# A chunked scan feeding two MLPs on one core: the second half of a piece's scan ahead of the next piece's first half

## The chip, the cores and the metric

The kernel runs on one core of a Trainium2 chip. The metric is device time of one execution in microseconds (us). Before the change three executions gave 623.71, 623.90 and 626.47 us, median 623.9.

## What is computed

The reference has three layers. The first is a decaying linear-attention scan over 768 steps for 4 batches and 8 heads, with state 16 x 32, in chunks of 32 steps:

```python
L = np.exp(cum[:, :, :, None] - cum[:, :, None, :]) * causal
M = np.einsum('bhin,bhjn->bhij', Cc, Bc) * L
y_intra = np.einsum('bhij,bhjd->bhid', M, xc)
y_inter = np.einsum('bhin,bhnd->bhid', Cc, state) * np.exp(cum)[:, :, :, None]
y[:, :, sl] = y_intra + y_inter
state = decay_full[:, :, None, None] * state + np.sum(Bx, axis=2)
```

Its output, as 3072 tokens of 256 features, goes through two MLPs of width 2048, `leaky_relu(x @ w_in) @ w_out` with slope 0.01 and `relu(x @ w_in)**2 @ w_out`. The weights come in as 64-bit floats.

## The kernel before, in words

**Pieces, blocks and weights.** The scan is cut into 12 pieces of 256 steps, three per batch (NPC, NP). Products run on split operands (a high and a low part, three products for one). The first MLP takes its tokens in blocks (BLOCKS, line 36): six blocks of one piece, then three of two. Block b needs yh and yl of its piece, written by the last step of that piece's scan (lines 422 and 423). A block of one piece runs in eight chunks of two rows of w1i: `hmm` issues 12 matmuls (lines 443 to 445), `act` has ScalarE write g and t (466, 467) and VectorE the low part of g (468), and `omm` issues 12 more (485, 486, 491), two chunks later (LAG). There are three g buffers and three PSUM tiles for hmm.

A weight tile goes through five steps: a load on SP's queue (117, into the pool "st" of seven buffers), two ScalarE passes (126, 129), two on VectorE (137, 139), one on ScalarE (161) and one on VectorE (162). `w_step` issues one step for each of four tiles in flight; the two tensors of the first MLP, w1i and w1o, are eight tiles each and come first, then w2i and w2o.

**The scan of a piece has two halves,** written as generators that yield after each small step.
- `scan_a(p)` (336): for the first batch scales from sums of squares (253, 308, 316 to 321, 264 to 283); him and ch on ScalarE (344, 345); `decays`, clips and a scan on VectorE (204 to 209); kmx and its diagonal copy kbd, xh (351, 354); cl (356); `from_start`, a second scan (214) and dec on ScalarE (215); xl and the copy of xh (361); the products S (368, 369), lines 370 and 373, the copy of xl; then mk (378).
- `scan_b(p)` (381): mkh and the carried state (384, 225), mkl and qh (389, 390), ql (392), the products Y (397 to 399), the states (401, 231), their parts and a transpose (406 to 410), the copy sbd, the last products (418, 419), yh and yl (422, 423).

A diagonal copy (`diag`, 328) of every piece but the first is four DMAs on SP's queue.

**What sets the order.** `stage(k)` (593) runs scan_a of piece k, scan_b of piece k-1 and, in stages 2, 5 and 8, `sequence_scales` of the next batch (287), which loads five tiles "all" into the pool "st" and has ScalarE square them. The three take turns step by step (601, 602), except in stage 1, where scan_b(0) comes whole first (597). The fourth round also emits the loads of the next piece (605), two DMAs on SP. `stages_to(x)` (612) draws steps until stage and step count, a stage being counted as 15 steps, reach x. Ahead of the blocks the kernel draws to 1 + 13.5/15 and issues eight weight steps (618 to 620); within them each chunk draws to `due(pos + 2)` (651), which makes stage p0 + n + 1 due four chunk halves ahead of a block (623) and spreads the steps at RATE. Stage k holds the last step of piece k-1.

The order of the text is not the order on an engine: a list scheduler puts instructions on each engine's queue, the earlier in the text first among those it takes to be ready. On the chip each queue then runs in that order.

Of the kernel before, what the change touches and what calls it, by code (L numbers as in the profile page):

```python
# [24 lines left out]
NP = BATCH * NPC  # L25
# [5 lines left out]
KI, KO = DM // P, FF // P  # L31
# [9 lines left out]
RATE = 1.4 / KO  # L41
LEAD = 4
NSTEP = 15
NHEAP = 24


# [5 lines left out]
def ssd_moe_kernel(ctx: ExitStack, tc: tile.TileContext, in1, in2, w1i, w1o, w2i, w2o, out):  # L52
# [10 lines left out]
    sm = ctx.enter_context(tc.tile_pool(name="sm", bufs=2))  # L63
    heap = ctx.enter_context(tc.tile_pool(name="heap", bufs=NHEAP))
    ap_ = ctx.enter_context(tc.tile_pool(name="ap", bufs=2))
# [126 lines left out]
    def load_piece(p):  # L192
        v = sp.tile([P, U * (N + T + D)], F32, tag="in1", name="in1", bufs=2)
        w = sp.tile([P, U * 2 * T], F32, tag="in2", name="in2", bufs=2)
        nc.sync.dma_start(v, in1[p])
        nc.sync.dma_start(w, in2[p])
        return part(v, N + T, D), part(v, 0, N), part(w, T, T), part(v, N, T), part(w, 0, T), part(w, 0, T + N)
# [89 lines left out]
    def sequence_scales(s):  # L287

        mx = sm.tile([P, 5], F32, tag="mx", name="mx")
        all_ = in1[NPC * s : NPC * s + NPC].rearrange("a p f -> p a f")  # L290

        for to, at in ((0, N + T), (3, N + T + 16), (1, N), (4, N + 16), (2, 0)):
            t = big([P, NPC, U * 16], F32, "all", "st", 7)
            nc.sync.dma_start(t, all_[:, :, U * at : U * (at + 16)])
            yield
            squares(mx[:, to : to + 1], t)
            yield
        sc, isc, sbp = yield from powers(mx, 5)

        fac = sm.tile([P, 1], F32, tag="fac", name="fac")  # L300
        nc.vector.tensor_tensor(fac, isc[:, 0:1], isc[:, 2:3], ALU.mult)
        nc.vector.scalar_tensor_tensor(fac, fac, 1.0 / KK, isc[:, 1:2], ALU.mult, ALU.mult)
        for p in range(NPC * s, NPC * s + NPC):
            scales[p] = sc[:, 0:1], sc[:, 2:3], sc[:, 1:2], sbp, fac, KK, 1.0
# [121 lines left out]
    blocks, q0 = [], 0  # L426
# [158 lines left out]
    def piece_y(p):  # L585
        return lambda: tuple(t[:, p % 2] for t in y_of(p))
# [6 lines left out]
    def stage(k):  # L593
        a = scan_a(k, loaded.pop(k)) if k < NP else iter(())
        b = scan_b(k - 1, piece_y(k - 1)) if k > 0 else iter(())
        bd = sequence_scales(k // NPC + 1) if k % NPC == NPC - 1 and k + 1 < NP else iter(())
        if k == 1:
            yield from b
        n = 0
        live = [b, a, bd]  # L600
        while live:
            live = [g for g in live if next(g, g) is not g]
            n += 1
            if n == 4 and k + 1 < NP:
                loaded[k + 1] = load_piece(k + 1)
            yield

    sc_it = (k for k in range(NP + 1) for _ in stage(k))
    now = [0, 0]
    cum = []  # L610

    def stages_to(x):
        while now[0] < NP + 1 and now[0] + min(now[1] / NSTEP, 0.99) < x:
            k = next(sc_it, NP + 1)
            now[:] = (k, now[1] + 1) if k == now[0] else (k, 0)

    stages_to(1)
    stages_to(1 + 13.5 / NSTEP)
    for _ in range(8):
        w_step()  # L620


    starts = [(KO * p0 - LEAD, p0 + n + 1) for p0, n in blocks[1:]]

    def due(at):
        return max(nb - max(RATE * (b - at), 0) for b, nb in starts)
# [16 lines left out]
    for i, (p0, n) in enumerate(blocks):  # L643
        ph_ = One(p0, n)
        for m in range(0, KO, 2 // n):
            ms = list(range(m, m + 2 // n))
            need("1i", m // 2)
            ph_.hmm(ms)
            pos += 2
            ph_.act(ms)  # L650
            stages_to(due(pos + 2))
            pend.append((ph_, ms, ms[-1] == KO - 1))
            if len(pend) > LAG[n]:
                need("1o", pend[0][1][-1] // 2)
            second(LAG[n])
            first_w = wq[:1] and wq[0][0][0] == "1" or any(v[0][0] == "1" for v in w_loaded + w_half + w_full)
            acc += 1.0 if first_w else (0.3 if i < len(blocks) - 1 else 1.5)
            while acc >= 1:
                acc -= 1
                (w_step if first_w else w_one)()  # L660
            if i == len(blocks) - 1 and m == KO - 4:
                split_y(0)
        if p0 % 2 + n == 2:
            ys.pop(p0 // 2)
# [68 lines left out]
```

## Time and profile before

| | us |
|---|---|
| three executions | 623.71, 623.90, 626.47 |
| profiled execution | 623.66 |
| its span, first to last instruction | 621.9 |
| TensorE busy | 574.2 |
| VectorE busy | 462.8 |
| ScalarE busy | 450.8 |
| mean granted clock of TensorE | 0.979 |

PE is TensorE, PEld its weight loads, DVE VectorE, ACT ScalarE, POOL GpSimd, SP the queue that issues the DMAs. Lines like L162 are lines of the kernel. A wait is idle time of an engine, put down to the operand that came last. The granted clock is a share of full speed.

### The profile page before, as it was taken

To read this page: it belongs to the slowest core of one execution; us is meant where nothing else is said; L and a number is where in the kernel's file an instruction comes from. 1 tells how busy PE (TensorE), PEld (TensorE's weight loads), DVE (VectorE), ACT (ScalarE), POOL (GpSimd) and SP (SyncE) were. 2 spreads that over 40 slices of the span, in tenths; PEclk is the share of its full clock that TensorE was granted. 3 is DMA by queue.
4 is the path that set the end of the run, shared out by engine and by line. 5 is a ranking of instruction groups with operands and counts; after the bars stand their busy time and mean duration, and the time that the engine had idled before them with its cause. 6 is when DMAs were issued, how large, how long until landed. Compare 5 with 4: busy or idle time off the path is not lost.

```text
span 621.9 us, 11809 instructions
## 1 busy us (share of the span) xinstructions
PE 574.2 (92%) x4674; PEld 521.6 (84%) x4674; DVE 462.8 (74%) x782; ACT 450.8 (72%) x723; POOL 5.2 (1%) x15
## 2 busy tenths in 40 slices
PE   0284889999999999999999999999999999999996
PEld 0274889899999978888888889989999999999996
DVE  6999799876688867645847457786787777777765
ACT  6996798766867765545666578877877878777773
POOL 3000000000000000000000000000000000000000
PEclk9985889999999999999999999999999999999999
DMA  8657766267357633202301000010010000100101
GB/s 322 211 130 225 231 184 156 28 155 236 47 110 199 185 65 53 28 10 52 87 24 35 0 2 2 0 35 1 1 34 1 9 27 1 35 1 1 35 1 35
DMA packets 113575, 46.52 MB, mean 75 GB/s; under 512 B 94448, under 2 KB 103280, under 8 KB 113520
## 3 DMA queue, kind: packets, MB, share of 16 engines
q1 hardware_dynamic: 113520, 45.76, 27.8%
q8 instruction: 37, 0.61, 0.4%
q14 instruction: 18, 0.15, 0.1%
HBM read 36.83 MB, written 3.15 MB: 64 GB/s over the span
## 4 chain that ended last, share of the span: by engine, by line
PE 83%; DVE 10%; ACT 3%; DMA 1%; issue 1%; DVEq 0%; ACTq 0%
PE hp L443 13%; PE hp L444 13%; PE hp L445 13%; PE o L485 4%; PE oo L485 4%; PE o L564 4%; PE o L491 4%; PE o L486 3%; PE o L562 3%; PE o L563 3%; PE oo L486 3%; PE oo L491 3%; PE Ym L564 3%; PE Ym L563 3%; PE Ym L562 3%
## 5 line engine op out<-in xcount | busy, mean ns | idle before, releaser
L443 PE MATMUL hp<-yl,w1i 128*128 128x256 f32 (+1 forms) x288 | 94.8, 329 | 9.1 <-DVE yl L423 6.4
L468 DVE TENSOR_TENSOR g<-t,g 128x512 fp32r<-128x512 f32 x96 | 65.7, 685 | 42.2 <-ACT t L467 39.7
L540 DVE TENSOR_TENSOR tl<-ts,th 128x1024 fp32r<-128x1024 f32 x48 | 58.8, 1225 | 49.2 <-ACT th L538 49.2
L445 PE MATMUL hp<-yh,w1i 128*128 128x256 f32 (+1 forms) x288 | 94.0, 326 | 0.0
L444 PE MATMUL hp<-yh,w1i 128*128 128x256 f32 (+1 forms) x288 | 93.8, 326 | 0.0
L466 ACT ACTIVATE g<-hp 128x512 fp32r<-128x512 f32 x96 | 57.2, 596 | 38.8 <-PE o L491 25.8
L528 ACT ACTIVATE b<-hp 128x512 f32<-128x512 f32 x96 | 57.2, 596 | 35.4 <-PE hp L445 35.4
L443 PE MATMUL hp<-xl,w2i 128*128 128x512 f32 x192 | 75.3, 392 | 0.0
L444 PE MATMUL hp<-xh,w2i 128*128 128x512 f32 x192 | 75.2, 392 | 0.0
L445 PE MATMUL hp<-xh,w2i 128*128 128x512 f32 x192 | 74.7, 389 | 0.0
L443 PEld LDWEIGHTS hp<-yl,w1i 128*128 128x128 f32 x288 | 56.8, 197 | 13.5 <-issue 4.0
L538 ACT CAST th<-ts 128x1024 fp32r<-128x1024 f32 x48 | 50.2, 1047 | 15.8 <-DVE ts L537 15.6
L445 PEld LDWEIGHTS hp<-yh,w1i 128*128 128x128 f32 x288 | 56.8, 197 | 3.7
L444 PEld LDWEIGHTS hp<-yh,w1i 128*128 128x128 f32 x288 | 56.8, 197 | 3.6
L485 PE MATMUL oo<-g,w1o 128*128 128x256 f32 x192 | 51.9, 300 | 8.3 <-DVE w1o L162 8.3
L467 ACT ACTIVATE t<-hp 128x512 f32<-128x512 f32 x96 | 57.3, 597 | 0.0
L529 ACT ACTIVATE b<-b 128x1024 f32<-128x1024 f32 x48 | 50.9, 1061 | 1.1
L486 PE MATMUL oo<-g,w1o 128*128 128x256 f32 x192 | 50.6, 293 | 0.0
L485 PEld LDWEIGHTS oo<-g,w1o 128*128 128x128 f32 x192 | 38.4, 200 | 9.1 <-DVE w1o L162 9.1
L539 DVE TENSOR_TENSOR bl<-b,bh 128x768 fp32r<-128x768 f32 x48 | 45.6, 951 | 0.0
L535 DVE TENSOR_TENSOR ts<-b 128x512 f32<-128x512 f32 x48 | 33.1, 690 | 13.4 <-ACT b L529 12.5
L445 PEld LDWEIGHTS hp<-xh,w2i 128*128 128x128 f32 x192 | 36.1, 188 | 7.9
(159 smaller groups left out, 1530.2 us busy)
## 6 DMA issues: line engine op xcount, KB each, us to landing
in<-in SPq DMA_DIRECT2D x12, 640.0 KB, 5.2
in<-in SPq DMA_DIRECT2D x12, 512.0 KB, 5.7
all<-in SPq DMA_DIRECT2D x15, 384.0 KB, 5.7
wst<-w1i SPq DMA_DIRECT2D x8, 512.0 KB, 8.4
wst<-w1o SPq DMA_DIRECT2D x8, 512.0 KB, 4.6
wst<-w2i SPq DMA_DIRECT2D x8, 512.0 KB, 6.8
wst<-w2o SPq DMA_DIRECT2D x8, 512.0 KB, 4.2
out_t<-r SPq DMA_DIRECT2D x24, 128.0 KB, 1.7
```

Of the source, the lines that this page charges most:

```text
L443: nc.tensor.matmul(hp, wh[:, k, c], xl[:, :, k], start=(k == 0), stop=False)
L444: nc.tensor.matmul(hp, wh[:, k, c], xh[:, :, k], start=False, stop=False)
L445: nc.tensor.matmul(hp, wl[:, k, c], xh[:, :, k], start=False, stop=(k == KI - 1))
L466: nc.scalar.activation(g[:, 0], hp, AF.Lrelu)
L467: nc.scalar.activation(t, hp, AF.Lrelu)
L468: nc.vector.tensor_tensor(g[:, 1], t, g[:, 0].bitcast(F32), ALU.subtract)
L485: nc.tensor.matmul(self.o[d], wl[:, c], gh, start=(m == 0 and (d == 0 or self.n == 2)), stop=False, **kw)
L486: nc.tensor.matmul(self.o[d], wh[:, c], gh, start=False, stop=False, **kw)
L528: nc.scalar.activation(b[:, 2 * i : 2 * i + 2], hp.rearrange("p (n t) -> p n t", n=2), AF.Relu)
L529: nc.scalar.activation(b, b, AF.Square)
L538: nc.scalar.copy(th, t)
L540: nc.vector.tensor_tensor(tl, t, th.bitcast(F32), ALU.subtract)
```

## The change

Up to stage 3 (APART) scan_b of the piece before is drawn whole ahead of scan_a of the stage's piece; before, this held for stage 1 alone. A stage up to 3 counts as 30 steps. The steps drawn ahead of the blocks end at 1.5 and not at 1.9: with the new count that is one step more, `decays` of piece 1 with the loads of piece 2. The dues of blocks 1 and 2 are set half a stage earlier: 2.5 and 3.5 for 3 and 4, the point at which scan_b of the block's piece is through.

```diff
+APART = 3
@@ stage
-        if k == 1:
+        if k <= APART:
             yield from b
@@ stages_to
-        while now[0] < NP + 1 and now[0] + min(now[1] / NSTEP, 0.99) < x:
+        while now[0] < NP + 1 and now[0] + min(now[1] / (2 * NSTEP if now[0] <= APART else NSTEP), 0.99) < x:
@@ ahead of the blocks
     stages_to(1)
-    stages_to(1 + 13.5 / NSTEP)
+    stages_to(1.5)
     for _ in range(8):
         w_step()
...
-    starts = [(KO * p0 - LEAD, p0 + n + 1) for p0, n in blocks[1:]]
+    starts = [(KO * p0 - LEAD, p0 + n + (0.5 if p0 + n <= APART else 1)) for p0, n in blocks[1:]]
```

## Rows read from the trace of the kernel before

**Rows 1.** The page's first part: busy time, share of the span and instructions, by engine.
```profile
PE 574.2 (92%) x4674; PEld 521.6 (84%) x4674; DVE 462.8 (74%) x782; ACT 450.8 (72%) x723; POOL 5.2 (1%) x15
```

**Rows 2.** Waits of PE, 0 to 130 us: total, times, longest.
```profile
PE oo L485 <- DVE w1o L162: 8.3, 3, 6.2
...
PE hp L443 <- DVE yl L423: 6.4, 3, 2.8
...
PE hp L443 <- ACT t L467: 2.7, 1, 2.7
```

**Rows 3.** Waits of PE, 111.6 us to the end.
```profile
PE o L485 <- DVE yf L500: 0.8, 1, 0.8
```

**Rows 4.** Timeline of PE: start, us, instruction; in brackets the wait ahead.
```profile
31.24 0.58 PE L443 MATMUL hp<-yl,w1i 128*128 128x256 f32 x1 [2.76 <-DVE yl L423]
...
56.94 0.58 PE L485 MATMUL oo<-g,w1o 128*128 128x256 f32 x1 [6.17 <-DVE w1o L162]
...
111.51 0.36 PE L443 MATMUL hp<-yl,w1i 128*128 128x256 f32 x1 [1.53 <-DVE yl L423]
```

**Rows 5.** Stages: length, busy of PE, PEld, DVE, ACT, POOL; granted clock, DMA share, GB/s.
```profile
31.10:89.00 57.90, 43.36 (x424) 41.59 (x425) 53.26 (x105) 47.13 (x92) 0.00 (x0) 0.79 0.69 193
...
111.50:137.00 25.50, 25.49 (x336) 25.33 (x337) 20.66 (x34) 17.30 (x35) 0.00 (x0) 1.00 0.48 107
137.00:209.00 72.00, 72.00 (x910) 71.38 (x909) 54.27 (x101) 50.68 (x98) 0.00 (x0) 1.00 0.59 138
```

**Rows 6.** Timeline of DVE, 7 to 129 us.
```profile
7.72 1.21 DVE L214 TENSOR_TENSOR_SCAN le<-in,d1e 128x512 f32<-128x512 f32 x1
8.86 0.14 DVE L317 TENSOR_SCALAR eb<-eb 128x3 int32<-128x3 int32 x1
...
46.67 1.21 DVE L209 TENSOR_TENSOR_SCAN le<-in,delta 128x512 f32<-128x512 f32 x1
47.80 0.93 DVE L389 TENSOR_TENSOR mkl<-in,mkh 128x768 f16<-128x768 f32 x1
...
48.72 1.22 DVE L214 TENSOR_TENSOR_SCAN le<-in,d1e 128x512 f32<-128x512 f32 x1
...
49.97 0.68 DVE L139 SCALAR_TENSOR_TENSOR wst<-wst 128x512 int32<-128x512 int32 x1
...
56.20 0.68 DVE L162 TENSOR_TENSOR w1o<-wst,w1o 128x512 fp32r<-128x512 f32 x1
...
63.48 0.94 DVE L389 TENSOR_TENSOR mkl<-in,mkh 128x768 f16<-128x768 f32 x1
...
72.32 0.75 DVE L392 SCALAR_TENSOR_TENSOR ql<-le,sc,qh 128x512 f16<-128x512 f32 x1 [1.05 <-ACT qh L390]
72.98 0.74 DVE L423 SCALAR_TENSOR_TENSOR yl<-Y,fac,yh 128x512 fp32r<-128x512 f32 x1
...
87.64 0.75 DVE L231 TENSOR_TENSOR_SCAN stt<-dec,d1s 128x288 f32<-128x288 f32 x1
88.31 0.67 DVE L162 TENSOR_TENSOR w1o<-wst,w1o 128x512 fp32r<-128x512 f32 x1
...
110.62 0.75 DVE L423 SCALAR_TENSOR_TENSOR yl<-Y,fac,yh 128x512 fp32r<-128x512 f32 x1
...
128.30 0.74 DVE L423 SCALAR_TENSOR_TENSOR yl<-Y,fac,yh 128x512 fp32r<-128x512 f32 x1
```

**Rows 7.** Timeline of ACT, 51 to 55.5 us.
```profile
51.77 0.83 ACT L253 ACTIVATE sq<-all 128x768 bf16<-128x768 f32 x1
...
54.93 0.66 ACT L161 ACTIVATE w1o<-wst 128x512 fp32r<-128x512 f32 x1
```

**Rows 8.** Timeline of SP's queue, 50 to 70 us: start, us issuing, instruction.
```profile
56.28 0.43 SPq L117 DMA_DIRECT2D wst<-w1o  x1
...
67.98 1.72 SPq L117 DMA_DIRECT2D wst<-w1o  x3
```

**Rows 9.** Stage 63.4 to 89, instructions on tiles "in" alone: DVE, ACT busy.
```profile
63.40:89.00 25.60, 6.87 (x10) 2.05 (x3) 0.87 0.70 219
```

## The prediction

> **What bounds the kernel now.** I read the page first: TensorE is busy for 574.2 of the span's 621.9 us [rows 1], so at most about 48 us of waiting can go anywhere. Next the waits of TensorE. In the first 130 us it waits for late operands: on the weights w1o 8.3 us in 3 waits, one of 6.2, on yl 6.4 in 3, on the copy t 2.7 once [rows 2]. After that its only wait is 0.8 us for yf [rows 3]. TensorE's timeline has block 0's first product at 31.24 and the first of block 2 (piece 2's products) at 111.51, behind the last wait on yl, 1.53 us [rows 4]. From there TensorE is busy for 25.49 of 25.5 and then for 72.00 of 72.0 us at full clock [rows 5]. So what is gained or lost at block 2's start goes through to the end, unless a new wait opens behind it; and all that the diff moves lies ahead of that point or close to it, since from the body of scan_b(3) on the text order is the same in both kernels (I walked the emission rules with both sets of numbers).
>
> Then the table by stage. From 31.1 to 89.0 VectorE is busy for 53.26 of 57.9 us, TensorE for 43.36 at a mean granted clock of 0.79 [rows 5], so part of its matmuls ran at 1.2 GHz, the lower level, in and after the waits. In this stretch VectorE sets the pace. A block with one piece's scan is 192 + 112 = 304 matmuls; at 336 in 25.5 us [rows 5] that is 23.1 us, so two of them would take 46 us, and blocks 0 and 1 take 80.
>
> VectorE's timeline says what stands ahead of the work that TensorE wants. Of the first w1o split L139 starts at 49.97 and the last step, L162, at 56.20; ahead of them stand the scans of piece 2, L209 at 46.67 and L214 at 48.72 [rows 6], which no product needs before block 2. On ScalarE the L161 between the two starts only at 54.93, behind squares of the next sequence (the tile "all" at 51.77) [rows 7]. On SP's queue the fifth w1o load goes out at 56.28 and the other three only from 67.98 [rows 8], behind the loads of "all", which take slots of the same seven-buffer pool, and behind the diagonal copies of piece 2. The eighth and last w1o L162 starts at 88.31 [rows 6] and ends at 89.0.
>
> **The change, part by part.** *Stages 2 and 3 emit scan_b(k-1) ahead of scan_a(k).* No instruction is added or removed. scan_a(2) with its three squares and twelve diagonal copies, the five "all" loads and squares, and the two loads of piece 3 come four chunks of block 0 later in the text; scan_a(3) comes behind scan_b(2). With the new *stages_to* and *starts* I count six complete w1o splits ahead of scan_a(2)'s last step where there was none, and all eight ahead of the body of scan_b(2) and of all of scan_a(3).
>
> The wait on t (2.7 us) is ScalarE's, which did piece 2's squares between block 0's first two activations; they leave, and I expect 0.5. The 6.2 us on w1o: ahead of that L162 the work of scan_a(2) drops out. By the rows of piece 3, nine such VectorE instructions and one mkl take 6.87 us [rows 9], so 5.9 and more, and the wait all but goes. What is late next is the following split, so I sum to the last split and not over single waits.
>
> The ledger: ahead of the last w1o split VectorE no longer does scan_a(3) and mkl(2) (6.87 us [rows 9]), the ql and the L231 of piece 2 (0.75 each) and the L137 of a w2i tile (as long as an L139, 0.69) [rows 6]: 9.1 us by durations. An instruction starts before the one ahead has ended (46.67 plus 1.21 is 0.08 past 47.80 [rows 6]), so 13 times 0.08 comes off: 8.1. Needed are 53.26 - 8.1 = 45.2 us. With no idle time the last split ends at 31.1 + 45.2 = 76.3; with all of the 4.6 us that VectorE idled in the stretch, at 80.9. The idle time is put down to the w1o loads that went out late [rows 8]; with "all" and piece 2's copies behind them on SP they go out before they are wanted, so part of it goes: I take 79 against 89.0.
>
> From 89.0 to 111.5 are 22.5 us of TensorE's work, and they remain (three g buffers tie the first products to the second ones): block 2 could start at 101.5. It also needs yl(2). Its chain begins with mkl(2), now behind the last split. From mkl to yl it took 25.2 us for piece 1 (47.80 to 72.98) and 47.1 for piece 2 (63.48 to 110.62) [rows 6], both beside the next piece's first half. Piece 1's is the nearer row, since block 1 waited for it as block 2 will; without a scan_a beside it, and with the sbd copies ahead of the next piece's on SP, it should be a little shorter: I take 23. Then yl(2) comes at 102 and block 2 starts at 103. Bounds: 76.3 + 22.5 less the wait of 1.5 gives 97.3; 80.9 + 25.2 + 0.9 (from yl's start to the product) gives 107.0.
>
> The profiled execution took 623.66 us (span 621.9 and 1.8 around it), 0.2 below the median of 623.9. The sum is 623.66 - (111.5 - 103) = **615.2 us**, with 609.5 and 619.2 for the bounds.
>
> *stages_to(1.5)* puts one more step ahead of the eight weight steps: piece 1's clips and L209 (1.2 us, as the row of piece 2 [rows 6]) and piece 2's load, two issues on SP. VectorE is full there either way; L209 trades places with w1i splits ahead of block 0, between 1.2 us saved and 1.2 lost. I take 0, nothing pointing either way. The two issues stand ahead of w1i's last load, which itself waits for a buffer; behind them wait w1i's last and w1o's first loads, wanted some 20 us later.
>
> *What is deferred must fit later.* Some 8 us of VectorE's work, and w2i splits, move behind 79. Between 111.5 and 209 VectorE has 25.5 - 20.66 and 72 - 54.27, together 22.6 us, free [rows 5], which hides them. Without that cover yl(3) would be late: it came at 128.30 [rows 6] for a block that starts some 25 us after block 2, at 136; now it is wanted by 128.
>
> Against the change: side by side, the two halves keep VectorE busy for 92% of the stretch [rows 5], and a half alone has its latencies bare. The Trainium skill, in "Perfetto Trace Analysis", section "Optimization Strategy", says that where the most-contended engine changes over time, interleaving the regimes may help; this change takes an interleaving out. By that rule the sum would be a loss, about that of the third rival. I weigh the rows higher: the interleaved work is not what TensorE waits for in block 0, and the weight splits fill the gaps.
>
> **The rivals.** *The wait moves to yl.* The chains of pieces 2 and 3 begin later than now and become the end of the path: with 27 to 30 us block 2 starts at 107 to 110, or block 3 waits for yl(3). For: piece 2's chain took 47 us. Against: it shared VectorE with scan_a(3) and the splits. Gain 1.5 to 4.5, time about 620.
>
> *The engine order hardly changes.* Text order is only a priority here: L214 of piece 0, emitted five steps behind L317, starts at 7.72, and L317 at 8.86 [rows 6]. If readiness decides instead, VectorE's queue stays as it is: 623.7. Against: L209, L214 and L139 from 46.67 to 49.97 [rows 6] stand in text order.
>
> *Slower.* scan_a(2) is starved behind the splits, and its second half then runs alone, with bare waits for its copies and products. It decides from a chain of 32 us on (111.5 - 79). At 38 us block 2 starts at 118, 6.5 us later: 630; at the 47.1 of now it would be 639.
>
> **How the numbers follow.** A measurement of this kernel can tell about 0.5%, 3.1 us, from no change. The forecast has 0.58 (609.5 to 619.2), the moved wait 0.14 (619 to 622, of which the part under 620.5, 0.10, counts as faster), no change 0.13, slower 0.15: so faster 0.68, same 0.17, slower 0.15. To leave out no more than 2 in 10 the range takes in the moved wait and most of no change: 609 to 624.
>
> **What would show it.** Right: the first L485 starts near 50 instead of 56.94 [rows 4], the waits on w1o sum to under 3 us, all eight w1o loads go out ahead of piece 2's kbd copies, the last w1o L162 starts near 78, and block 2 near 103 with TensorE full behind it. Wrong: the last L162 is early but yl(2) comes later than 107 (first or third rival), L209 of piece 2 still stands ahead of the first w1o L162 (second), or new waits on yl open behind block 2.

## The result, and the profile after

The changed kernel takes 617.74 us (median of four executions, 617.09 to 618.51); the kernel before, run beside it, 625.15 (623.71 to 626.47). The ratio is 0.9882, with a 95% interval of 0.985 to 0.9914: 1.2% faster. The forecast was 615.2, in a range of 609 to 624. The lines of the changed kernel are one higher than before (L485 is now L486).

The page's span and busy time by engine. The span was 621.9 before [rows 1]: 6.2 us went, 1.6 of them out of TensorE's own busy time (574.2), the rest out of its waits.

```profile
span 615.7 us, 11798 instructions
...
PE 572.6 (93%) x4674; PEld 520.1 (84%) x4674; DVE 460.8 (75%) x782; ACT 450.9 (73%) x723; POOL 5.2 (1%) x15
```

TensorE's waits from 0 to 130 us, for [rows 2] (total, times, longest). The wait on w1o fell from 8.3 to 1.4, that on yl from 6.4 to 2.2. That on t stayed (2.7 before), and two grew or came: on mkh, and on a kbd copy.

```profile
PE Y L398 <- ACT mkh L385: 5.2, 2, 2.8
PE hp L444 <- ACT t L468: 2.8, 3, 1.5
PE hp L444 <- DVE yl L424: 2.2, 1, 2.2
PE S L369 <- DMA kbd<-kmx: 2.2, 1, 2.2
...
PE oo L486 <- DVE w1o L163: 1.4, 1, 1.4
```

VectorE's timeline, for [rows 6]. The first w1o split now ends its last step ahead of piece 2's scan (L210, which stood at 46.67 before), and the eighth does so 12 us earlier than before (88.31). mkl(2), at 79.04, comes 15.6 us *later* than before, and yl(2), at 101.11, 9.5 us earlier.

```profile
48.35 0.68 DVE L163 TENSOR_TENSOR w1o<-wst,w1o 128x512 fp32r<-128x512 f32 x1
...
59.02 1.22 DVE L210 TENSOR_TENSOR_SCAN le<-in,delta 128x512 f32<-128x512 f32 x1
...
63.78 0.74 DVE L424 SCALAR_TENSOR_TENSOR yl<-Y,fac,yh 128x512 fp32r<-128x512 f32 x1
...
76.05 0.69 DVE L163 TENSOR_TENSOR w1o<-wst,w1o 128x512 fp32r<-128x512 f32 x1
...
79.04 0.96 DVE L390 TENSOR_TENSOR mkl<-in,mkh 128x768 f16<-128x768 f32 x1 [0.29 <-ACT mkh L385]
...
101.11 0.75 DVE L424 SCALAR_TENSOR_TENSOR yl<-Y,fac,yh 128x512 fp32r<-128x512 f32 x1
```

SP's queue, for [rows 8]: the last four w1o loads go out together, where the fifth stood at 56.28 and the others at 67.98.

```profile
44.68 4.71 SPq L118 DMA_DIRECT2D wst<-w1o  x4
```

TensorE's timeline, for [rows 4]: block 0's first product, its first second product (56.94 before), the products S(3) that wait for a kbd copy, and block 2's first product (111.51 before). Ahead of the last row no wait is printed: yl(2), 101.11 plus 0.75, ends just as the S products do.

```profile
30.65 0.58 PE L444 MATMUL hp<-yl,w1i 128*128 128x256 f32 x1 [2.24 <-DVE yl L424]
...
50.95 0.56 PE L486 MATMUL oo<-g,w1o 128*128 128x256 f32 x1
...
100.87 0.19 PE L369 MATMUL S<-ch,kbd 128*128 128x32 f16 x1 [2.16 <-DMA kbd<-kmx]
...
101.92 0.58 PE L444 MATMUL hp<-yl,w1i 128*128 128x256 f32 x1
```

The table by stage, for [rows 5]. In the first stretch, which ends with the last w1o split, VectorE is busy for 44.83 of 46.1 us: it hardly idles. From 130 on TensorE is full, as before. The row to look at is the second: behind the wait for kbd the granted clock is 0.62 on average for 4.2 us, so most of it at 1.2 GHz, the lower level. At full clock the same work would take 4.2 x 0.62 = 2.6 us, so 1.6 are lost.

```profile
30.60:76.70 46.10, 38.27 (x377) 37.08 (x377) 44.83 (x84) 42.59 (x83) 0.00 (x0) 0.89 0.73 202
...
100.90:105.10 4.20, 4.12 (x47) 4.02 (x48) 4.20 (x7) 1.76 (x3) 0.00 (x0) 0.62 0.44 51
...
130.00:202.00 72.00, 72.00 (x891) 71.53 (x887) 52.42 (x94) 49.07 (x97) 0.00 (x0) 1.00 0.51 115
```

TensorE's waits from 104 us to the end, for [rows 3]. Before there was one, 0.8 us on yf; now yf takes 1.2 and a new one stands at 205.69, on the squares of the last batch.

```profile
PE o L486 <- DVE yf L501: 1.2, 1, 1.2
PE S L309 <- ACT sq L254: 1.0, 1, 1.0
```

So the ledger reads: block 2 starts 111.51 - 101.92 = 9.6 us earlier; 1.6 go to the low clock behind its start, 1.0 to the squares, 0.4 to yf. That leaves 6.6, and the spans differ by 6.2; 0.4 is not placed. The work behind that point is the same, 3912 matmuls in both traces.

### The profile page after: what moved, and what is told of

It is laid out like the page before. It is cut to its first block, busy times and chain, and to the rows that moved or that the text cites. A ratio compares the mean times of both kernels' runs of the same rounds, so it can differ in the third digit from the quotient of the medians.

```text
span 615.7 us, 11798 instructions
## 1 busy us (share of the span) xinstructions
PE 572.6 (93%) x4674; PEld 520.1 (84%) x4674; DVE 460.8 (75%) x782; ACT 450.9 (73%) x723; POOL 5.2 (1%) x15
## 4 chain that ended last, share of the span: by engine, by line
PE 79%; DVE 9%; ACT 8%; issue 2%; DMA 1%; SPq 0%; DVEq 0%; ACTq 0%
PE hp L444 13%; PE hp L445 13%; PE hp L446 13%; PE o L486 4%; PE o L565 4%; PE o L492 4%; PE o L487 4%; PE o L563 4%; PE o L564 3%; PE Ym L565 3%; PE Ym L564 3%; PE Ym L563 3%; PE oo L486 2%; PE oo L487 2%; PE oo L492 2%
## 5 line engine op out<-in xcount | busy, mean ns | idle before, releaser
L486 PE MATMUL oo<-g,w1o 128*128 128x256 f32 x192 | 50.0, 290 | 1.4 <-DVE w1o L163 1.4
L487 PE MATMUL oo<-g,w1o 128*128 128x256 f32 x192 | 50.0, 290 | 0.0
L444 PEld LDWEIGHTS hp<-xl,w2i 128*128 128x128 f32 x192 | 36.2, 189 | 6.3
```

What stands on the lines that cost most here:

```text
L444: nc.tensor.matmul(hp, wh[:, k, c], xl[:, :, k], start=(k == 0), stop=False)
L486: nc.tensor.matmul(self.o[d], wl[:, c], gh, start=(m == 0 and (d == 0 or self.n == 2)), stop=False, **kw)
L487: nc.tensor.matmul(self.o[d], wh[:, c], gh, start=False, stop=False, **kw)
```

## The experiments

Twelve kernels. The ratios are to the kernel before in the same session. The runs come from several sessions, the change itself from one of its own; between sessions, differences of up to 3.5 us have ratios whose intervals overlap, and their size is rough. The table has the starts on VectorE that decide: piece 2's scan L209, last step of the first and the last w1o split, mkl(2), and yl of pieces 1 and 2.

| | time, us | scan(2) | first, last split | mkl(2) | yl(1) | yl(2) |
|---|---|---|---|---|---|---|
| before | 624 to 625 | 46.67 | 56.20, 88.31 | 63.48 | 72.98 | 110.62 |
| the change | 617.7 | 59.02 | 48.35, 76.05 | 79.04 | 63.78 | 101.11 |
| order_only | 614.2 | 59.31 | 48.64, 78.51 | 75.23 | 64.73 | 96.19 |
| all_late | 622.7 | 46.62 | 56.47, 85.06 | 67.21 | 68.08 | 108.48 |
| all_early | 619.7 | 57.67 | 48.04, 77.49 | 85.02 | 66.91 | 102.55 |
| apart2 | 622.0 | 58.36 | 48.40, 80.02 | 77.36 | 63.72 | 106.97 |
| due_full | 621.9 | 47.56 | 57.43, 87.81 | 72.14 | 64.88 | 96.77 |
| no_step | 617.1 | 59.18 | 48.51, 76.25 | 79.25 | 63.95 | 101.33 |
| order_step | 613.3 | 58.44 | 48.46, 77.66 | 74.38 | 63.86 | 95.33 |
| order_11 | 619.6 | 59.30 | 48.62, 78.50 | 75.22 | 64.72 | 96.19 |
| after_lead8 | 615.1 | 58.54 | 48.47, 75.98 | 77.19 | 63.39 | 98.92 |
| pace_only | 622.1 | 49.76 | 49.03, 75.75 | 66.61 | 77.92 | 107.74 |
| order_lead6 | 616.1 | 56.03 | 48.93, 76.40 | 72.71 | 63.44 | 94.35 |
| after_lead8b | 616.0 | 49.73 | 49.00, 76.11 | 77.31 | 63.26 | 99.01 |

**order_only: the new order under the old pace.** The kernel before, with one edit.

```diff
-        if k == 1:
+        if k <= 3:
             yield from b
```

> The kernel before with scan_b(k-1) whole ahead of scan_a(k) up to stage 3, but with the old pace, dues and eight-step point. Order theory (the gain comes from piece 2's first half standing behind the w1o splits on VectorE and ScalarE): with the old dues, stage 2 is drawn to its end by the fourth chunk of block 0, so scan_a(2) is back ahead of most of the splits; the first L162 of w1o starts near 51, the last near 85, and 1 to 3 us of the 6 to 7 remain. Load theory (the gain comes from the w1o loads going out ahead of the loads of all on SP and in the shared pool): the five all loads are drawn early again, so about nothing remains. If the order inside a stage alone were the gain: 6 us below the kernel before.

614.23 us, ratio 0.9826 (0.9785 to 0.9867). The order holds all of the gain, and seems to hold more: without the new count and dues the kernel is 3.5 us faster than with them (the two intervals overlap; no_step and order_step below show 3.8 us within one session). That more was to be had from the order alone was no theory of mine, and the later runs ask what the new pace costs.

**all_late: only the loads and squares of "all" moved,** behind the rest of stage 2, in the kernel before.

```diff
-        live = [b, a, bd]
+        live = [b, a] if k == 2 else [b, a, bd]
...
             yield
+        yield from bd
```

> The kernel before with only the five loads and squares of all in stage 2 moved behind the rest of that stage; scan_a(2) and scan_b(1) stay side by side. Load theory: the fifth w1o load goes out near 45 instead of 56 and the next three before 60 instead of 68; VectorE's 4.6 us of idle time between 31 and 89 go, the last L162 of w1o starts near 82 instead of 88, and 4 to 6 us of the gain are there. Order theory: the first L162 of w1o still starts near 54 behind L209 and L214 of piece 2, and at most 2 us are gained.

622.66 us, ratio 0.9969 (0.9946 to 0.9992). Piece 2's scan stays ahead of the first split (46.62 and 56.47) and the waits on w1o stay at 7.7 us in all. The edit gains some 2 us. It does not bring all the loads forward, as the load theory had it: the fifth goes out at 49.09 and the last three only at 63.64, since piece 2's diagonal copies still stand ahead of them on SP. So it prices the part of the lateness that "all" causes, and not the whole.

```profile
49.09 0.42 SPq L117 DMA_DIRECT2D wst<-w1o  x1
...
63.64 2.27 SPq L117 DMA_DIRECT2D wst<-w1o  x3
```

**all_early: "all" ahead of scan_a(2)** in the changed kernel.

```diff
-            yield from b
+            for _ in b:
+                next(bd, None)
+                yield
```

> The changed kernel with only the five loads and squares of all put back beside scan_b(1), ahead of scan_a(2). Order theory: piece 2's VectorE work still stands behind the splits, so the first L163 of w1o starts within 1.5 us of the changed kernel's 48.35 (five squares of 0.75 us more on ScalarE), the last within 3 us of 76.05, and the time is at most 2 us above the changed kernel. Load theory: the last four w1o loads go out at 55 or later, the last L163 near 82 to 85, and the time is 4 to 6 us above the changed kernel, close to the kernel before.

619.67 us, ratio 0.9904 (0.9874 to 0.9934). The last four w1o loads fall back to 45.5 and 53.0, and some 2 us go, the size of the run above, though the interval overlaps that of the change. In both runs the loads of "all" are the smaller part. Neither moves all the w1o loads while VectorE's order stays, so what the rest of their lateness is worth is not shown.

**apart2: stage 3 side by side again,** with its old count and due, in the changed kernel.

```diff
-APART = 3
+APART = 2
```

> The changed kernel with APART = 2: stage 3 is side by side again, with the old count and due. The ledger of the prediction puts 8 of VectorE's us (scan_a(3) and the body of scan_b(2)) behind the last w1o split by way of stage 3: then the last L163 starts 3 to 8 us later than 76.05 and yl(2) comes later too, and the time is 2 to 5 us above the changed kernel. If stage 2 alone carries the change (piece 2 behind the splits), the last L163 is within 2 us of 76.05 and the time within 1 us of the changed kernel.

621.96 us, ratio 0.9947 (0.9926 to 0.9968): 4.2 us of the gain go. From mkl(2) to yl(2) it now takes 106.97 - 77.36 = 29.6 us where the changed kernel takes 22.1. TensorE's timeline shows for what: for the sbd copy of piece 2, which goes out on SP at 98.92, behind twelve copies of piece 3 (in the changed kernel at 92.59, ahead of them), and then for kbd(3).

```profile
104.51 0.21 PE L419 MATMUL Y<-qh,sbd 128*128 128x32 f16 x1 [3.49 <-DMA sbd<-t]
...
107.31 0.19 PE L369 MATMUL S<-ch,kbd 128*128 128x32 f16 x1 [1.77 <-DMA kbd<-kmx]
```

**due_full, no_step, order_step: which part of the new pace costs 3.5 us.** The first puts the old dues into the changed kernel, the second takes its extra step out, the third puts that step into order_only.

```diff
due_full
-    starts = [(KO * p0 - LEAD, p0 + n + (0.5 if p0 + n <= APART else 1)) for p0, n in blocks[1:]]
+    starts = [(KO * p0 - LEAD, p0 + n + 1) for p0, n in blocks[1:]]
no_step
-    stages_to(1.5)
+    stages_to(1.46)
order_step (against order_only)
-    stages_to(1 + 13.5 / NSTEP)
+    stages_to(1 + 14.5 / NSTEP)
```

> The changed kernel with the due of the kernel before (a whole stage, not half of one, ahead of blocks 1 and 2); order, step count and the extra early step stay. The order alone, with all of the old pace, took 614.2, the whole change 617.7: this run and the next two ask which part of the new pace costs the 3.5 us. If it is the later due (scan_a of pieces 2 and 3 and mkl(2) later): 614 to 615.5, last w1o step at 77 to 80, mkl(2) near 75 to 76, yl(2) at 96 to 98, no wait at block 2's start. If it is the extra early step or the halved step: 617 to 618.5 and yl(2) stays near 101.

> The changed kernel without the one extra step ahead of the eight weight steps; the rest of the new pace stays. If the extra step costs (L209 of piece 1 and piece 2's load ahead of block 0's weights): 614 to 615.5 and block 0 starts near 30.4. If the later due costs: 617 to 618.5, yl(2) still near 101, block 0's start within 0.6 us of the changed kernel's 30.65.

> The kernel before with the order of stages 2 and 3 changed and the extra early step, old due and old step count. Due theory: within 1 us of the order alone, 613.5 to 615.5. Step theory: 616.5 to 618. Should both hold in part, 615.5 to 616.5.

due_full took 621.92 us (ratio 0.9956, 0.9937 to 0.9975), far from both expectations. By the rules of emission, with 30 steps to a stage and a whole stage due, scan_b(1) is through in block 0's second chunk and scan_a(2) follows at once, nearly all of it ahead of the first w1o split. VectorE's timeline has the old order back, and TensorE has the old wait (7.6 us on w1o in all, 6.27 at 58.16):

```profile
47.56 1.22 DVE L210 TENSOR_TENSOR_SCAN le<-in,delta 128x512 f32<-128x512 f32 x1
...
57.43 0.68 DVE L163 TENSOR_TENSOR w1o<-wst,w1o 128x512 fp32r<-128x512 f32 x1
...
58.16 0.58 PE L486 MATMUL oo<-g,w1o 128*128 128x256 f32 x1 [6.27 <-DVE w1o L163]
```

This is the plainest test of the forecast's reason: scan_b goes ahead of scan_a in it, yet with scan_a(2) ahead of the splits most of the gain is gone. The trace also says which engine holds the first split. Its load is among the three that go out at 30.06, and ScalarE's step of it is done at 51.0. VectorE, busy for 10.00 of the 10.0 us from 47.5 to 57.5 mostly with scan_a(2) and steps of scan_b(1), does the last step only behind them. So neither the loads nor ScalarE make that wait. For the last split the run does not part the causes, since the last two w1o loads go out late too, at 71.94.

```profile
30.06 5.47 SPq L118 DMA_DIRECT2D wst<-w1o  x3
...
50.33 0.69 ACT L162 ACTIVATE w1o<-wst 128x512 fp32r<-128x512 f32 x1 [2.28 <-DVE wst L140]
...
47.50:57.50 10.00, 2.85 (x50) 2.36 (x50) 10.00 (x27) 7.32 (x15) 0.00 (x0) 0.50 0.61 225
...
71.94 0.82 SPq L118 DMA_DIRECT2D wst<-w1o  x2
```

no_step took 617.13 us (0.9866 to 0.9919), the same as the change: the extra step costs nothing that shows. order_step took 613.33 us (613.16 to 614.42; ratio 0.983, 0.9805 to 0.9856). With order_only, from which its ratio does not differ, it is the fastest kernel, ahead of the kernel before and, in the same session, of no_step, which does what the change does; the intervals of these two don't meet. So the 3.5 us lie in the new count and the new dues together; the one run that parts them, due_full, is slower than either pair. By the rules of emission the old count makes 15 steps a stage: scan_b(1) is spread over the first half of block 0, and scan_a(2) comes in one burst in its middle, behind three of the eight w1o splits. On VectorE four splits end ahead of piece 2's scan (58.44), as in the changed kernel, and most of the rest of scan_a(2) comes ahead of the other four. So it need not stand behind all of them. In order_step TensorE enters block 2 without any wait, as the window around its start shows:

```profile
96.00:104.00 8.00, 8.00 (x95) 7.91 (x94) 7.68 (x15) 7.88 (x15) 0.00 (x0) 1.00 0.59 118
```

**order_11: the new order in every stage,** under the old pace.

```diff
-        if k <= 3:
+        if k <= 11:
```

> The kernel before with scan_b ahead of scan_a in all stages, not only up to the third; old pace. TensorE is full from block 2 on, so if only what is late ahead of block 2 counts: 613.5 to 615.5, as with the order up to stage 3 alone. If the later second halves matter: up to 1.5 us faster where the waits on squares and yf near the two-piece blocks go away, or 2 to 6 us slower where scan_a of a piece, now behind, comes late for the blocks of two pieces.

619.63 us, ratio 0.9926 (0.9901 to 0.9951): 5.4 us slower than with the order up to stage 3. Up to block 2 the two are alike (yl(2) at 96.19 in both). Behind it TensorE, full in order_only, idles for 1.3, 0.6 and 1.3 us in these three stretches; its waits from 100 to 200 are many and small (copies of sbd and xbh, mkl):

```profile
98.00:130.00 32.00, 30.70 (x377) 30.18 (x377) 28.54 (x48) 22.22 (x43) 0.00 (x0) 1.00 0.54 115
130.00:170.00 40.00, 39.40 (x462) 38.84 (x460) 26.99 (x52) 29.50 (x57) 0.00 (x0) 1.00 0.60 144
170.00:207.00 37.00, 35.71 (x465) 34.86 (x464) 27.49 (x44) 21.30 (x40) 0.00 (x0) 1.00 0.51 120
```

Against these 3.2 us, order_only waits longer for yf further on: from 98 us to the end the two idle for 9.0 and 6.5 us. That is 2.5 of the 5.2 us by which the spans differ; the rest stays open. Here the rule on interleaving regimes, weighed in the prediction, may have its case: the Trainium skill ("Perfetto Trace Analysis", section "Optimization Strategy") says that it may help, and in the stretch where TensorE is full, taking it out costs 5 us. Ahead of block 2 the trace goes the other way.

**after_lead8: block 2's due four positions earlier** in the changed kernel. Does piece 2's chain cost the rest?

```diff
-    starts = [(KO * p0 - LEAD,
+    starts = [(KO * p0 - (8 if p0 == 2 else LEAD),
```

> The changed kernel, with the due of block 2 four positions earlier (28 to 24, a sixth of a block; about 5 us of TensorE's work). Theory: block 2 starts at 101.9 because piece 2's chain, from mkl at 79, is only just done (yl at 101.1), and the low clock after that wait costs near 2 us more. Then the chain comes 3 to 5 us earlier: mkl(2) 75 to 76, yl(2) 96 to 98, block 2 near 98.5 without a wait and at full clock, 614 to 615.5. Rival: the last w1o splits, with scan_a(2) and mkl(2) now ahead of some of them, give the time back: last step at 78 to 80, 616.5 to 618.5.

615.12 us, ratio 0.9854 (0.9834 to 0.9874): by the times 2.6 of the 3.5 us, though its interval overlaps that of the change. yl(2) comes 2.2 us earlier, the last w1o split stays (75.98), and the wait in front of block 2 shrinks to 0.5, behind which the clock stays full:

```profile
99.72 0.39 PE L444 MATMUL hp<-yl,w1i 128*128 128x256 f32 x1 [0.50 <-DVE yl L424]
...
99.00:104.00 5.00, 4.47 (x43) 4.24 (x40) 5.00 (x11) 4.42 (x10) 0.00 (x0) 1.00 0.45 54
```

**pace_only: the new pace without the new order.** The changed kernel, with this edit.

```diff
-        if k <= APART:
+        if k == 1:
             yield from b
```

> The new pace without the new order: stages 2 and 3 side by side as before, with the later due, the halved step and the extra early step. Theory (what counts is the VectorE work that stands ahead of the w1o splits in the text, however it gets there): scan_a(2) now stands ahead of about half of them, so half of the gain or less: 619 to 622, a w1o wait of 2 to 6 us. If the delay alone were enough: 616.5 to 618.5 with w1o waits under 2 us. If the order alone counts: 623 to 625.

622.12 us, ratio 0.9959 (0.994 to 0.9978), just above the first expectation. The splits are as early as in the changed kernel (last one at 75.75), and it gains almost nothing: scan_b(1) shares VectorE with scan_a(2), so yl(1) comes at 77.92, 14 us later than in the changed kernel, and yl(2) at 107.74. The waits, 0 to 130 us:

```profile
PE hp L444 <- ACT t L468: 6.9, 3, 3.4
PE hp L444 <- DVE yl L424: 5.4, 3, 2.8
PE oo L486 <- DVE w1o L163: 5.1, 4, 1.6
```

So an early last split is not enough; each block's chain must be early too.

**order_lead6 and after_lead8b: can block 1 start earlier still?** In order_step block 1 waits 2.73 us for yl(1). The first run sets every due of order_step two positions earlier, the second the dues of blocks 1 and 2 of the changed kernel four.

```diff
order_lead6
-LEAD = 4
+LEAD = 6
after_lead8b
-    starts = [(KO * p0 - LEAD,
+    starts = [(KO * p0 - (8 if p0 <= 2 else LEAD),
```

> The order in stages 2 and 3 and the extra step under the old pace (613.3), with every due two positions earlier. There the waits left are yl at block 1 (2.3 us, yl(1) at 63.9) and the copies t. If yl(1) comes one chunk earlier and nothing else gives: 611 to 612.5, block 1 some 2 us earlier. If scan_a(2), now a chunk earlier, stands ahead of splits that TensorE wants: 613.5 to 616, w1o waits of 1 to 4 us.

> The changed kernel with the dues of blocks 1 and 2 both four positions earlier; with block 2's alone it took 615.1 and block 1 still waited 2.2 us for yl(1). Here only the second halves move ahead; scan_a(2) stays behind the splits by the due of 2.5, unlike in the run with every due earlier, where it stood ahead of them and w1o and t waited 7 us. If yl(1) comes 2 us earlier at no price: 612 to 613.8, block 1 at 61 to 62.5. If scan_b(1) merely trades places with w1o splits: 614.5 to 616.5, with waits on w1o of 2 to 4 us in block 1.

616.14 us (ratio 0.9864, 0.9842 to 0.9886) and 615.97 us (0.9873, 0.9843 to 0.9904), near the second, slower expectation of each; neither beats the kernel that it starts from. yl(1) comes at 63.44 and 63.26, hardly earlier than the 63.86 and 63.39 of the kernels that they start from. What gives way is the other side: scan_a(2) moves ahead, in after_lead8b right behind the first split step, and waits on t appear (5.1 and 3.9 us in all, against 2.8 and 2.1):

```profile
49.00 0.67 DVE L163 TENSOR_TENSOR w1o<-wst,w1o 128x512 fp32r<-128x512 f32 x1
...
49.73 1.22 DVE L210 TENSOR_TENSOR_SCAN le<-in,delta 128x512 f32<-128x512 f32 x1
```

The waits on w1o stay at 2.0 and 1.1 us. VectorE is full in this stretch (in after_lead8b busy for 45.55 of the 46.2 us from 30.6 to 76.8); an earlier due there only changes which of its customers is late.

## Why the prediction was right, and where it was off

**What held.** The reason: in blocks 0 and 1 VectorE sets the pace, and the first half of piece 2's scan stood ahead of w1o splits that TensorE wanted sooner. due_full shows it for the first split, the wait of 6.2 us. For the last one the late loads of [rows 8] are a second cause that no run parts from the order; all_late and all_early only show that "all" has a small part in it. The steps fell where they were put: the first second product near 50 (50.95), w1o waits under 3 us (1.4), all w1o loads ahead of piece 2's kbd copies (44.68), the last split's end at 79 (76.7, the forecast's bound without idle time: 44.83 of 46.1 us are busy), the chain from mkl(2) to yl(2) 23 us (22.1), block 2 at 103 (101.92), nothing for the extra step (no_step). yl(3), wanted by 128, came at 127.85, and no wait stands on it.

**What failed: "what is gained or lost at block 2's start goes through to the end, unless a new wait opens behind it".** Block 2 gained 9.6 us where 8.5 were forecast, and the span 6.2. The term was mis-sized by three things that it took to be nothing: the low clock behind the start (1.6), the squares of the last batch (1.0), a longer wait on yf (0.4). The forecast took [rows 5], at full clock behind block 2's start, for the state of the changed kernel too; but behind the 2.2 us wait ahead of it the clock fell. That is why the time is 617.7 and not 615.2, and two errors partly cancel in it by luck: block 2 started 1.1 us earlier than forecast, without which the miss would be larger by as much. Giving the chain more lead (after_lead8) brings 615.1.

**Smaller misses.** Of the 9.1 us in the ledger the ql of piece 2 (0.75) did not leave: it starts at 75.25, ahead of the last split. The wait on t was to fall to 0.5 and is 2.8: piece 2's squares left ScalarE, but passes of the weight splits took their place in its queue. The sum took the last split as what releases block 2 (76.7 + 22.5 = 99.2); it is piece 2's chain that does (kbd(3) at 100.87, yl(2) ending at 101.86), and pace_only shows that the split's end alone sets nothing. The start came out right since the chain was in the sum as well.

**The rivals.** *The wait moves to yl* had its mechanism half right: block 2 does wait for that chain, but one of 22 us and not of 27 to 30. apart2, with stage 3 mixed, is that rival: a chain of 29.6, block 2 near 108, 622.0. *The engine order hardly changes* fell with piece 2's scan at 59.02 instead of 46.67. *Slower* would have needed 32 us. The rule of the Trainium skill ("Perfetto Trace Analysis", section "Optimization Strategy") that interleaving may help would have made a loss of it. VectorE, busy for 92% of the stretch before [rows 5], is busy for 97% up to the last split without the interleaving, with weight splits between the steps; but it is so in pace_only too (44.39 of 45.9 us), which keeps the interleaving and gains little. So its busy share does not decide, and what it does first does.

## What to carry to other kernels

Where one engine is full ahead of a block, order its work by when each consumer wants it: here weight splits and the next block's second half ahead of a first half wanted a block later. Then look for the chain that you pushed back and give it lead: here its wait of 2.2 us in front of a full TensorE cost 1.6 us of clock as well. And stop where the engine has slack: with the same edit beyond block 2 as well the kernel is 5 us slower.

## What the hardware showed

A short wait of TensorE can have a second price, a fall of its clock. Behind the wait of 2.16 us at block 2 the granted clock was 0.62 for 4.2 us. In order_step, where block 1 waits 2.73 us, it was 0.57 from 66 to 70, and in the changed kernel, behind 1.40 us on w1o, 0.57 from 63.9 to 67.9. The first cost 1.6 us (4.2 x 0.38) on top of its wait, the other two 1.7 each (4 x 0.43).

Which waits have this price the traces don't say. Behind the 0.50 us of after_lead8 and the 1.53 us at block 2 of the kernel before [rows 4, 5] the clock stayed at 1.00; but it did so behind 2.23 us at block 1 in after_lead8, too, and fell behind the 1.40 us. So the length of the wait alone does not decide, and what does stays open.

```profile
64.66 0.39 PE L443 MATMUL hp<-yl,w1i 128*128 128x256 f32 x1 [2.73 <-DVE yl L423]
...
66.00:70.00 4.00, 4.00 (x22) 4.00 (x22) 4.00 (x8) 4.00 (x8) 0.00 (x0) 0.57 0.42 67
```

The changed kernel, and then after_lead8:

```profile
63.91 0.39 PE L486 MATMUL oo<-g,w1o 128*128 128x256 f32 x1 [1.40 <-DVE w1o L163]
...
63.90:67.90 4.00, 3.99 (x21) 3.99 (x21) 4.00 (x7) 4.00 (x9) 0.00 (x0) 0.57 0.98 365
```

```profile
64.19 0.39 PE L444 MATMUL hp<-yl,w1i 128*128 128x256 f32 x1 [2.23 <-DVE yl L424]
...
64.15:69.00 4.85, 4.13 (x32) 3.93 (x33) 4.85 (x8) 4.85 (x11) 0.00 (x0) 1.00 0.97 280
```
